# Transformer layers in one kernel: the PSUM banks of the projections divided five to three, and more score maxima computed there

## The chip, the cores and the metric

The kernel runs on one core of one Trainium2 chip. The metric is the device time of one execution in microseconds (us); the median of several runs is compared. An engine is named as in the profile: PE (TensorE matmul), PEld (its weight loads), DVE (VectorE), ACT (ScalarE), POOL (GpSimd) and SP (SyncE, which issues DMAs). PSUM, where PE puts its results, has eight banks of 128 x 512 fp32 each.

## The reference

One sequence of 2048 rows and 640 columns goes twice through an attention block and a dense block, with the same weights each time:

```
x = x + A(layernorm(x)); x = x + B(layernorm(x))     # twice
A: qkv = x @ wqkv; 32 heads of 20 columns each
   scores = q k^T / sqrt(20); p = softmax(scores over 2048 keys); (p v) @ wo
B: r = max(x @ w1 + b1, 0); (r * r) @ w2 + b2        # 1536 columns inside
```

The softmax needs, for each head and each query, the maximum over 2048 scores before the exponentials can be summed. The kernel computes it exactly, in a pass of its own.

## The kernel before

Each layer has three stages: the projections (`qkv`), attention (`attention`), and a dense stage (`add_heads`, `mlp`). Everything is written out in the order in which it is to run; each engine takes its instructions in that order and waits on semaphores where data or a bank is not ready.

**Projections.** There are 72 sums per layer: 40 for queries and keys (128 weight columns by 512 rows of x, named `("qk", tb, pos)`), then 32 for values (128 rows by 320 columns). Both operands are split in a high and a low part, so a sum takes 15 products (5 blocks of 128 x three combinations), and each product is cut in two halves of 64 rows of the array that work side by side, `r` 0 and 1. In `product` (L311) one half opens a sum with its 15 products, and the other half closes it with its own 15 into the same bank. A mark on ACT (L333) keeps the halves in order. In `work_on` (L893) the halves take turns: in each phase of 15 steps one half opens a sum while the other closes an earlier one, so that a sum opens in one phase, rests in the next, and is closed in the third. A sum gets its bank from the ring `ps_pj` (L97) when its first product is issued (L330). When it is closed, `end` (L859) has ACT read it: once (L263) or twice (L263 and L265) for queries and keys, once (L377) for values.

**Maxima in the projections.** Between these products `insert` (L810) puts matmuls of scores by queries (L481), whose maxima are needed later. They take their banks from the ring `ps_q` (L98). There are plain ones ("one": matmul, maximum on DVE, L493) and doubled ones, which deal with two blocks of keys at once: max(a, b) = b + relu(a - b). For these a first matmul with differences of keys goes through a relu on ACT ("step", L502), and a second is added to it, with the maximum, on DVE ("both", L510). A pair is put in only where a small model says that the next bank of the ring is free: `now` holds a clock for PE, DVE and ACT, `busy` a time for each bank, and `takes` (L768) advances them. The lists `PLAIN` and `DOUBLE` (L661, L667) say which blocks of queries and keys may be put in, and in what order; what does not fit by the end of the projections is left to attention.

**Attention.** A key tile of one block of 512 queries and 4 heads needs four score matmuls (L565, letters a and b for the two row halves), four exponentials on ACT (L572), and eight instructions on PE that sum the exponentials times the values (L577, letter V). The remaining maxima (L481, L493, letters m and n) are mixed in. `ORDERS` (L958) holds one order for each number of pairs of maxima in eight key tiles, 12 to 16; `pairs` (L1102) chooses the number from what is still due, at least 12.

Of the kernel before, what the change touches and what calls it, by code (L numbers as in the profile page):

```python
# [25 lines left out]
NQB = S // QB  # L26
# [13 lines left out]
def tile_layers(  # L40
# [53 lines left out]
            return [self.order[(self.n + 1 + i) % len(self.order)] for i in range(k)]  # L94

    ps_st = Ring(0, 1, 2, 3)
    ps_pj = Ring(4, 5, 6, 7)  # L97
    ps_q = Ring(0, 1, 2, 3)  # L98
    ps_all = Ring(0, 1, 2, 3, 4, 5, 6, 7)

    ident = cpool.tile([P, P], F32, name="ident")
# [321 lines left out]
    k_t, q_t, v_t, mx_t, kept = {}, {}, {}, {}, {}  # L423
# [65 lines left out]
    def smax(ring, t, p, sub, c, par):  # L489

        dst = ring("sm")
        by_queries(dst, t, p, sub, c, par)
        nc.vector.tensor_reduce(  # L493
            maxima(t)[:, 2 * par + p, sub, c : c + 1], dst, axis=AX.X, op=ALU.max
        )
# [58 lines left out]
    free = []  # L554
# [90 lines left out]
    def prep_job():  # L645
# [7 lines left out]
        if jobs:  # L653
# [16 lines left out]
        ([(0, 2, "d")], [(1, 2, "d")]),  # L670
        ([(0, 3, "d"), (0, 3, "e"), (0, 2, "e"), (0, 1, "e"), (0, 0, "e")],
         [(1, 3, "d"), (1, 0, "e"), (1, 1, "e"), (1, 2, "e"), (1, 3, "e")]
         + [(2, qb, c) for qb in range(NQB) for c in "de"]),
    ]
    PARTLY = {g * NQB + qb for x in DOUBLE for y in x for g, qb, c in y}

# [7 lines left out]
    def qkv(first, x_src, rest, scores):  # L684
# [5 lines left out]
        state = {"n": 0, "op": None, "last": "one", "scores": True}  # L690
        turning = []
        now = {"pe": 0.0, "dve": 0.0, "act": 0.0}
        busy = [0.0] * 8
# [8 lines left out]
        for pos in range(2 if first else FIRST, 10):  # L702
            n = UNITS.index((0, pos)) - 5 if pos >= FIRST else 0
# [9 lines left out]
        for k in range(KD if first else w_v.n):  # L713
            n = len(UNITS) - 8 + k
# [50 lines left out]
            while len(pending) > keep:  # L765
                pending.pop(0)()

        def takes(engine, ns, spot):  # L768
            now[engine] = max(now[engine], now["pe"] + 0.25) + ns
            busy[spot] = now[engine] + 0.12  # L770

        def choose():

# [12 lines left out]
        def single(op, par):  # L786

            (g, qb, x), p, sub = op["w"]
            t = g * NQB + qb
            spot = ps_q.coming(1)[0]  # L790
            if op["kind"] == "one":
                smax(ps_q, t, p, sub, x, par)
                takes("dve", 0.62, spot)
                keys_done = [x]
            elif op["kind"] == "step":
                op["r"].append(step_one(t, p, sub, x, par))
                takes("act", 0.58, spot)
                op["ready"].append(now["act"] - 0.2)
                return
            else:  # L800
                both_one(t, p, sub, x, par, op["r"][par])
                takes("dve", 0.7, spot)
                c = 2 * "de".index(x)
                keys_done = [c, c + 1]
            if par:
                done.update((t, p, sub, c) for c in keys_done)
                if (p, sub) == PAIRS[-1]:
                    end_group(op["w"][0])

        def insert(par):  # L810


            op = state["op"]
            if bool(op) != bool(par):
                return False
            if now["pe"] < max(busy[b] for b in ps_q.coming(1)):
                return False
            if turning and not par and now["pe"] >= turning[0][0]:
                if now["pe"] < max(busy[b] for b in ps_q.coming(2)):
                    return False  # L820
                now["pe"] += 1.2
                for spot in ps_q.coming(2):
                    takes("act", 0.6, spot)
                    takes("dve", 0.7, spot)
                step_turn()
                return False
            if not op:
                if min(at_now) >= (len(chains) - 1) * N + 2 * N // 3:
                    if state["scores"]:
                        state["scores"] = False  # L830
                        next(scores)
                    return False
                op = state["op"] = choose()
                if not op:
                    return False
                state["last"] = op["kind"]
            single(op, par)
            if par:
                state["op"] = None
            return True  # L840
# [8 lines left out]
        def step_turn():  # L849
            if next(turning[0][1], None) is None:  # L850
                turning.pop(0)
# [57 lines left out]
        for j in range(len(chains)):  # L909
# [18 lines left out]
            n = j - 2  # L928
# [31 lines left out]
        15: "anbmnanbaabmbnammbnaVbmbmmbVmbananVanmbanVnambmbVanbmnaVnmbaanVmbbanmV",  # L960
        14: "mbbbanmbbmambmVanannaVmbnaaanVbmabnmVanbmbmbVnaanmbVmabmbanVbmannaVn",
        13: "baanmbVmbanambbnbmVanbmnaVnaabnmbVanbmaanVnmbbanaVmnbmabVabbmmnaVm",
        12: "naambbmVanmbambVbmannabVnabnmabVabnmbanVbbmnanaVbmmbaanVbmbmnaaV",
    }

    def attention(first, x_src, first_rows):
# [4 lines left out]
        st_n, sm_n = [0, 0], [0, 0]  # L971
        state = {"begun": -1, "done": 0, "acc": None, "debt": 0}
        sm_ring = Ring(4, 5, 6)
        todo = [
            (t, p, sub, c)
            for t in range(NBLK)
            for c in range(4)
            for p, sub in PAIRS
            if (t, p, sub, c) not in done
        ]  # L980
# [13 lines left out]
        def begin(i):  # L994

            t, u = divmod(i, NKT)
            g, qb = divmod(t, NQB)
            if u == 1:
                q_t.pop(t - 1, None)
                if t + 2 < NBLK and t + 2 not in q_t:  # L1000
                    load_q(t + 2)
            if u % 4 == 1 and qb == 0:
                k_t.pop((g - 1, u // 4), None)
                for h in (0, 1, 2, 3) if g else (0, 1, 2):
                    if g + h < NG and (g + h, u // 4) not in k_t:
                        load_k(g + h, u // 4, True)
                if g and g + 3 >= NG:
                    del kept[(g - 1) % 4, u // 4]
            if t == 1 and u % 4 == 1:
                load_k(3, u // 4, True)  # L1010
            if u in (2, 10) and qb == NQB - 1 and g + 1 < NG:
                load_v(g + 1, u // 8)
            if first and t < 16 and u % 6 == 3:
                prep_job()
            if first and t < 16 and u == 8:
                for sp in (w_o, w_1, w_2):
                    sp.save_full()
                    sp.past(sp.count, sp.got)
            if (t, u) in loads:
                loads[t, u]()  # L1020
            if t == NBLK - 1 and u == 12:
                first_rows.extend(row_tile(x_src, i) for i in range(4))
            if i in split:
                split.pop(i)()
# [77 lines left out]
        def pairs():  # L1102

            n, i = min(sm_n), state["begun"] + 1
            most = max(
                [8 * (e + 1 - n) / max(t * NKT - 3 - i, 1) for t, e in ends.items() if e >= n],
                default=0,
            )
            state["debt"] += most
            n = min(max(int(state["debt"]), 12), 16)  # L1110
            state["debt"] -= n
            return n

        free.extend((5, 6))
        for o in "abab":
            op(o)
        yield
# [2 lines left out]
        spare = 0  # L1120
        while state["done"] < wide:
            for o in ORDERS[pairs()]:
# [3 lines left out]
                        both_heads(spare // 2 - 1)  # L1126
                else:
                    op(o)
        assert min(sm_n) == len(todo) and spare == 4
        for p in (0, 1, 0):  # L1130
            both_heads(p)
        while state["done"] < last:
# [11 lines left out]
    ready = {}  # L1144
# [348 lines left out]
```

## Time and profile before

| | |
|---|---|
| median of 3 runs | 3582.21 us (3581.59 to 3583.35) |
| profiled execution: span from first to last instruction | 3581.5 us (the page gives no other time for it) |
| granted PE clock | 1.000 |
| PE busy | 3569.0 us |
| DVE busy | 2753.5 us |
| ACT busy | 2647.3 us |
| POOL busy | 805.2 us |
| maxima matmuls L481 (plain and second of a doubled one; first of a doubled one) | 3586 of 427 ns, 510 of 400 ns |
| products of the projections L331 (queries and keys; values) | 2400 of 394 ns, 1920 of 307 ns |
| sums of attention L577 | 8192 of 605 ns |

A line "L331 PE" means instructions that line 331 of the kernel issued on PE. A busy time is the union of the spans of an engine's instructions. Matmuls overlap each other, since each is listed from its start to its result, so PE can be busy all the time without issuing at its fastest; the spacing of starts tells more. In the text, a window such as 700.00:790.00 is in us from the start of the span.

### The profile page before, as it was taken

The numbers are of one execution on the slowest core, as the hardware profiler recorded it, in microseconds if no ns is written. First come the engines' busy times: TensorE is split into PE (matmuls) and PEld (weight loads), VectorE is DVE, ScalarE is ACT, GpSimd is POOL, SyncE is SP. The second block draws the span as 40 slices with busy tenths as digits, with TensorE's granted clock in tenths as the row PEclk, the third lists the DMA queues.
The fourth block names the chain that finished last, engine by engine and source line by source line (L and its number), as shares of the span: only waits on it lengthen the run. The fifth ranks groups of instructions, "written<-read, shape, count | busy, mean of one in ns | idle before, by whom it ended". The sixth has DMA issues, their size and how long they took to land.

```text
span 3581.5 us, 67667 instructions
## 1 busy us (share of the span) xinstructions
PE 3569.0 (100%) x25560; PEld 2121.6 (59%) x25560; DVE 2753.5 (77%) x5085; ACT 2647.3 (74%) x5146; POOL 805.2 (22%) x880
## 2 busy tenths in 40 slices
PE   9999999999999999999999999999999999999999
PEld 7896343333334335999988954333334433369998
DVE  8778999999999993455567789999999999824443
ACT  3778999999999995122237789999999999942221
POOL 6531434211211211111153201211211211211110
PEclk9999999999999999999999999999999999999999
DMA  9765555323211136834477652232232211367221
GB/s 305 274 230 167 168 157 155 105 69 81 57 44 51 46 95 204 262 99 115 134 275 244 192 149 70 62 81 60 66 79 54 52 39 45 112 216 248 74 80 39
DMA packets 377397, 452.58 MB, mean 126 GB/s; under 512 B 176642, under 2 KB 223746, under 8 KB 377070
## 3 DMA queue, kind: packets, MB, share of 16 engines
q1 hardware_dynamic: 376254, 445.89, 41.6%
q8 instruction: 201, 3.29, 0.4%
q10 hardware_dynamic: 816, 2.36, 0.2%
q14 instruction: 126, 1.03, 0.1%
HBM read 273.83 MB, written 174.30 MB: 125 GB/s over the span
## 4 chain that ended last, share of the span: by engine, by line
PE 96%; DVE 2%; DMA 1%; issue 0%; ACT 0%; POOL 0%; SPq 0%; ACTq 0%; DVEq 0%
PE banks L577 28%; PE banks L565 20%; PE banks L481 16%; PE banks L293 13%; PE banks L331 10%; PE banks L1259 9%; DVE mx L493 1%; PE banks L1091 1%; DMA q<-d_qk 0%; ACT e L1098 0%; DVE bst L244 0%; DVE xnT L257 0%; DVE x L252 0%; DMA d_qk<-ev 0%; PE banks L408 0%
## 5 line engine op out<-in xcount | busy, mean ns | idle before, releaser
L572 ACT ACTIVATE e<-banks 128x512 f32<-128x512 f32 x3968 | 2049.4, 604 | 61.1 <-PE banks L481 1.7
L493 DVE TENSOR_REDUCE mx<-banks 128x1 f32<-128x512 f32 x3076 | 1929.6, 683 | 208.4 <-PE banks L481 137.2
L481 PE MATMUL banks<-k,q 60*128 60x512 f32 x3586 | 1244.3, 427 | 1.0 <-DMA q<-d_qk 0.5
L565 PE MATMUL banks<-q,k 62*128 62x512 f32 x3968 | 1118.7, 434 | 0.4 <-DVE mx L510 0.4
L577 PE MATMUL banks<-e,vg 128*32 128x512 f32 x8192 | 1091.0, 605 | 1.5 <-ACT e L1098 1.5
L565 PEld LDWEIGHTS banks<-q,k 62*128 62x128 f32 x3968 | 584.4, 185 | 657.8 <-ACT e L572 625.6
L481 PEld LDWEIGHTS banks<-k,q 60*128 60x128 f32 x3586 | 582.0, 184 | 283.1 <-DVE mx L493 210.8
L510 DVE CUSTOM_DVE_ANT_0 rl<-banks,rl 128x512 f32<-128x512 f32 x510 | 332.6, 688 | 101.6 <-PE banks L481 91.0
L331 PE MATMUL banks<-xnT,wqk 64*128 64x512 f32 x2400 | 379.7, 394 | 0.3 <-ACT mark_t L333 0.3
L1244 ACT ACTIVATE r<-banks,b_t 128x512 f32<-128x512 f32 x96 | 66.2, 689 | 419.7 <-PE banks L293 418.3
L577 PEld LDWEIGHTS banks<-e,vg 128*32 128x32 f32 x8192 | 161.1, 108 | 360.2 <-issue 333.1
L502 ACT ACTIVATE rl<-banks 128x512 f32<-128x512 f32 x510 | 270.8, 597 | 98.9 <-PE banks L481 93.6
L1259 PE MATMUL banks<-w,h 128*128 128x320 f32 x2304 | 340.4, 309 | 0.0
L1259 PEld LDWEIGHTS banks<-w,h 128*128 128x128 f32 x2304 | 339.2, 188 | 1.2
L293 PE MATMUL banks<-xnT,w 128*128 128x512 f32 x1440 | 329.4, 389 | 0.0
L331 PEld LDWEIGHTS banks<-xnT,wqk 64*128 64x128 f32 x2400 | 286.4, 185 | 34.3 <-issue 2.4
L293 PEld LDWEIGHTS banks<-xnT,w 128*128 128x128 f32 x1440 | 269.6, 188 | 55.3
L271 POOL CAST mr<-nt 128x32 fp32r<-128x32 f32 x64 | 13.4, 209 | 1143.5 <-DVE nt L536 1143.5
L621 POOL TENSOR_TENSOR few<-few,minus_t 128x16 f32<-128x16 f32 x62 | 179.8, 2900 | 215.6 <-DMA few<-d_s 213.7
L331 PE MATMUL banks<-wv,xnT 64*128 64x320 f32 x1920 | 199.2, 307 | 0.9 <-ACT mark_t L333 0.9
L331 PEld LDWEIGHTS banks<-wv,xnT 64*128 64x128 f32 x1920 | 186.5, 185 | 2.7 <-ACT mark_t L333 1.4
L1245 DVE TENSOR_TENSOR r<-r 128x512 f32<-128x512 f32 x96 | 74.3, 774 | 124.0 <-ACT r L1244 124.0
(86 smaller groups left out, 2010.8 us busy)
## 6 DMA issues: line engine op xcount, KB each, us to landing
q<-d_qk SPq DMA_DIRECT2D x242, 240.0 KB
d_qk<-ev SPq DMA_DIRECT2D x80, 512.0 KB
k<-d_qk SPq DMA_DIRECT2D x152, 240.0 KB
x<-d_x SPq DMA_DIRECT2D x84, 320.0 KB
d_qk<-ev SPq DMA_DIRECT2D x80, 256.0 KB
d_o<-ot SPq DMA_DIRECT2D x248, 80.0 KB
ot<-d_o SPq DMA_DIRECT2D x38, 512.0 KB
d_v<-v SPq DMA_DIRECT2D x32, 512.0 KB
```

The source lines that it names most:

```text
L293: nc.tensor.matmul(dst, a, b, start=(n == 0), stop=(n == last))
L331: m = nc.tensor.matmul(ch["dst"][:, :width], *pair, start=first, stop=last)
L481: nc.tensor.matmul(dst, q_t[t][b : b + 60, p, sub * P : (sub + 1) * P], k_t[t // NQB, c][b : b + 60, p, :], start=True, stop=True,)
L493: nc.vector.tensor_reduce(maxima(t)[:, 2 * par + p, sub, c : c + 1], dst, axis=AX.X, op=ALU.max)
L502: nc.scalar.activation(res, dst, AF.Relu)
L510: nc.vector.tensor_tensor_reduce(out=r, in0=dst, in1=r, scale=1.0, scalar=LEAST, op0=ALU.add, op1=ALU.max, accum_out=maxima(t)[:, 2 * par ...
L565: nc.tensor.matmul(dst, k_t[t // NQB, kt // 4][b : b + 62, p, (kt % 4) * P : (kt % 4 + 1) * P], q_t[t][b : b + 62, p, :], start=True, stop ...
L572: nc.scalar.activation(es[p][:, par, :], dst, AF.Exp, scale=SCALE)
L577: nc.tensor.matmul(acc[32 * h : 32 * h + 32, :], v_t[t // NQB, kt // 8][:, kt % 8, 32 * h : 32 * h + 32], es[p][:, par, :], start=(kt == 0 ...
L621: nc.gpsimd.tensor_tensor(few, few, minus_t, op=ALU.pow)
L1245: nc.vector.tensor_mul(r, r, r)
L1259: nc.tensor.matmul(dst[:, :HALF], hs[f][:, hx, i * P : (i + 1) * P], w_2.piece(at_2(f0 + f, hw, hf)), start=(f == 0 and (hx, hw) == THREE[0]),
```

## The change

It has four parts. The eight banks are divided anew: three (5, 6, 7) for the sums of the projections and five (0 to 4) for the maxima there. `DOUBLE` gets four more blocks (group 3, query blocks 0 and 1). The model behind `insert` charges an engine a spacing and a bank a whole duration, and begins no earlier than 0.44 us behind PE. And attention may choose ten or eleven pairs of maxima per eight key tiles, with an order for each.

```diff
-    ps_pj = Ring(4, 5, 6, 7)
-    ps_q = Ring(0, 1, 2, 3)
+    ps_pj = Ring(5, 6, 7)
+    ps_q = Ring(0, 1, 2, 3, 4)
...
-         + [(2, qb, c) for qb in range(NQB) for c in "de"]),
+         + [(2, qb, c) for qb in range(NQB) for c in "de"] + [(3, 0, "d"), (3, 0, "e"), (3, 1, "d"), (3, 1, "e")]),
...
-        def takes(engine, ns, spot):
-            now[engine] = max(now[engine], now["pe"] + 0.25) + ns
-            busy[spot] = now[engine] + 0.12
+        SPACING = {"dve": 0.60, "act": 0.48}
+        WHOLE = {"dve": 0.78, "act": 0.70}
+
+        def takes(engine, spot):
+            begins = max(now[engine], now["pe"] + 0.44)
+            now[engine] = begins + SPACING[engine]
+            busy[spot] = begins + WHOLE[engine]
+            return busy[spot]
...
-                takes("dve", 0.62, spot)
+                takes("dve", spot)
...
-                takes("act", 0.58, spot)
-                op["ready"].append(now["act"] - 0.2)
+                op["ready"].append(takes("act", spot) - 0.44)
...
-                takes("dve", 0.7, spot)
+                takes("dve", spot)
...
-                    takes("act", 0.6, spot)
-                    takes("dve", 0.7, spot)
+                    takes("act", spot)
+                    takes("dve", spot)
...
+        11: "ananmbbVmbanmabVmbabmnaVbabmnaVbmbmnaaVnabnmbaVnabanmbVabanmbV",
+        10: "anmbabVabmnmbaVmbabanVbmnanabV" * 2,
...
-            if t == 1 and u % 4 == 1:
+            if t == 1 and u % 4 == 1 and (3, u // 4) not in k_t:
...
-            n = min(max(int(state["debt"]), 12), 16)
+            n = min(max(int(state["debt"]), 10), 16)
...
-        free.extend((5, 6))
+        free.extend((ps_pj.coming(1)[0], 4))
...
-        assert min(sm_n) == len(todo) and spare == 4
+        assert min(sm_n) == len(todo) and spare >= 4, spare
```

The change moves instructions. The first place is PE in the first layer's projections of queries and keys, where one sum closes and the next opens. xnT is a block of the input, wqk of the weights; "waits Activation" is a semaphore of ACT. Before, the third last row closes a sum in bank 6, and the last row opens the next one in bank 5 (as the ring gives them out), with no wait:

```order
L331 MATMUL banks_74<-xnT53_456,wqk169_1592 128x512
L331 MATMUL banks_74<-xnT97_802,wqk169_1592 128x512
L481 MATMUL banks_74<-kd111_1005,q160_1522 128x512 [waits DVE_49]
L331 MATMUL banks_74<-xnT97_802,wqk169_1592 128x512
L331 MATMUL banks_74<-xnT53_456,wqk169_1592 128x512
L331 MATMUL banks_74<-xnT75_616,wqk139_1320 128x512
L331 MATMUL banks_74<-xnT24_251,wqk169_1592 128x512
```

Now, the second row closes a sum in bank 6, and the sixth opens the next one in the same bank, behind ACT's read of it:

```order
L481 MATMUL banks_74<-kd112_1012,q167_1559 128x512 [waits Activation_49]
L331 MATMUL banks_74<-xnT28_263,wqk180_1644 128x512
L331 MATMUL banks_74<-xnT80_642,wqk180_1644 128x512
L481 MATMUL banks_74<-k71_591,q167_1559 128x512 [waits Activation_49]
L331 MATMUL banks_74<-xnT47_419,wqk140_1332 128x512
L331 MATMUL banks_74<-xnT91_766,wqk140_1332 128x512 [waits Activation_49]
L481 MATMUL banks_74<-k71_591,q167_1559 128x512 [waits DVE_49]
```

Over both layers 138 sums open in a bank that an earlier sum of the same projections had. Before, 31 to 55 matmuls of PE lie from the closing one to the opening one, and 18 openers name a wait for such a read; now the distance is 2 for 88 of them, 4 for 43, 6 for 6 and 10 for one, and 135 openers wait for the read (L263, L265 or L377) of the bank that they open. Of the 138, 56 banks were read once for queries and keys (29 openers at distance 2, 26 at 4, 1 at 6), 24 twice (17, 4, 2, and 1 at 10), and 58 for values (42, 13, 3).

The maxima matmuls in the projections go from 572 to 678 in the first layer and from 576 to 680 in the second, all of the added ones doubled.

The second place is PE in attention, in the middle of the first layer. Before, each key tile has four scores (L565) and three maxima (L481) ahead of its sums (L577):

```order
L565 MATMUL banks<-q_9329,k_5325 128x512
L481 MATMUL banks<-k_4962,q_9476 128x512
L565 MATMUL banks<-q_9329,k_5325 128x512
L481 MATMUL banks<-k_4962,q_9476 128x512 x2
L565 MATMUL banks<-q_9329,k_5325 128x512 x2
L577 MATMUL banks<-e_4746,vg_8849 32x512 x2
L577 MATMUL banks<-e_4745,vg_8849 32x512 x2
```

Now some key tiles have two maxima:

```order
L565 MATMUL banks<-q_10154,k_4742 128x512 x3
L481 MATMUL banks<-k_5156,q_10161 128x512 x2
L565 MATMUL banks<-q_10154,k_4742 128x512
L577 MATMUL banks<-e_5028,vg_10341 32x512 x2
L577 MATMUL banks<-e_5027,vg_10341 32x512 x2
```

In each layer 104 key tiles now have two and 387 three, where 491 and 489 had three before. In groups of eight key tiles eleven and twelve pairs occur, ten does not. The other stages keep their instructions.

## The prediction

> **What bounds the kernel now.** I read the page first: busy time by engine and the chain of work that ended last.
>
> ```profile
> span 3581.5 us, 67667 instructions
> PE 3569.0 (100%) x25560; PEld 2121.6 (59%) x25560; DVE 2753.5 (77%) x5085; ACT 2647.3 (74%) x5146; POOL 805.2 (22%) x880
> PE 96%; DVE 2%; DMA 1%; issue 0%; ACT 0%; POOL 0%; SPq 0%; ACTq 0%; DVEq 0%
> PE banks L577 28%; PE banks L565 20%; PE banks L481 16%; PE banks L293 13%; PE banks L331 10%; PE banks L1259 9%; DVE mx L493 1%; PE banks L1091 1%; DMA q<-d_qk 0%; ACT e L1098 0%; DVE bst L244 0%; DVE xnT L257 0%; DVE x L252 0%; DMA d_qk<-ev 0%; PE banks L408 0%
> ```
>
> PE is the bound of every stage. Its modelled ends hide short gaps, so I then counted matmuls per stretch: one with projections of queries and keys, one with projections of values, one of attention (columns: PE, PEld, DVE, ACT, POOL, clock, DMA share, GB/s).
>
> ```profile
> 1870.00:1910.00 40.00, 40.00 (x337) 32.69 (x336) 32.40 (x96) 28.82 (x61) 18.36 (x19) 1.00 0.79 276
> 2030.00:2074.00 44.00, 44.00 (x538) 43.04 (x534) 32.68 (x102) 31.91 (x79) 2.09 (x5) 1.00 0.74 210
> 700.00:790.00 90.00, 90.00 (x640) 35.74 (x634) 81.79 (x135) 87.48 (x171) 16.21 (x15) 1.00 0.28 72
> ```
>
> In the projections a matmul starts every 40/337 = 0.119 us (512 columns) and every 44/538 = 0.082 us (values: 320 columns, mixed with maxima). Two row halves work side by side, so one lasts over three times the spacing:
>
> ```profile
> L331 PE MATMUL banks<-xnT,wqk x2400: 383/392/502, 12.3 to 1994.3; 64*128 64x512 f32 x185
> L331 PE MATMUL banks<-wv,xnT x1920: 299/306/413, 206.9 to 2090.5; 64*128 64x320 f32 x192
> ```
>
> There is hardly a stall in the projections to be filled. What is added to PE there costs time, and so does what makes PE wait there.
>
> **The change, part 1: three banks for the sums.** A sum (a chain, in the code) is opened by one row half, rests for a phase, and is closed by the other half. So during each phase one sum is open, one rests and one closes: three banks. With a ring of four, the next sum opens in the fourth while ACT reads the closed one. With three, it opens in the bank that has just been closed. The order shown ahead says how far opener and closer are apart: of the 138 openers that reuse a bank inside a projection, all but the first few now stand 2 (88 times), 4 (43), 6 (6) or 10 (1) matmuls behind the closer of the same bank, where they stood 31 or more before. 135 of them wait for ACT's read of that bank. PE takes its instructions in order, so all that stands behind waits too: the other half's products and the inserted maxima.
>
> How long is that wait? Here a closing run of products, the reads that follow it on ACT, and PE's answer to an ACT instruction at the end of attention, where PE visibly waits:
>
> ```profile
> 1834.51 0.86 PE L331 MATMUL banks<-xnT,wqk 64*128 64x512 f32 x5
> 1835.47 0.59 ACT L263 COPY r<-banks 128x512 f32<-128x512 f32 x1
> 1835.95 0.59 ACT L265 CAST ev<-banks 128x512 fp32r<-128x512 f32 x1
> ...
> 1391.78 1.43 ACT e L1098
> 1393.20 0.04 issue
> 1393.25 1.06 PE banks L577 x8
> ...
> L377 ACT COPY v<-banks x60: 409/426/449, 219.2 to 2085.6; 128x320 f32<-128x320 f32 x60
> ```
>
> The closer ends at 1834.51 + 0.86 = 1835.37, the read begins 0.10 us later and takes 0.59; a second read (the first four column blocks of the weights, in three of four row blocks) begins 0.48 later. PE answers 0.05 us after ACT's end. After a wait PE also loses about 0.10 us, since the first two pairs stand 0.34 us apart and not 0.235; this is seen behind every switch to attention's sums:
>
> ```profile
> 699.60 1.07 PE L577 MATMUL banks<-e,vg 128*32 128x512 f32 x8
> 700.59 0.50 PE L565 MATMUL banks<-q,k 62*128 62x512 f32 x1
> 700.93 0.39 PE L565 MATMUL banks<-q,k 62*128 62x512 f32 x1
> 701.17 0.62 PE L565 MATMUL banks<-q,k 62*128 62x512 f32 x2
> 701.72 1.07 PE L577 MATMUL banks<-e,vg 128*32 128x512 f32 x8
> ```
>
> So from closer's start to opener: 0.39 + 0.10 + 0.59 + 0.05 + 0.10 = 1.23 us with one read, 1.71 with two, and 0.31 + 0.10 + 0.43 + 0.05 + 0.10 = 0.99 for values. Taken off is what PE needs anyway over 2, 4 or 6 places.
>
> - One read, 56 openers: 29 x (1.23 - 0.24) + 26 x (1.23 - 0.48) + 1 x (1.23 - 0.71) = 28.7 + 19.5 + 0.5 = 48.7 us.
> - Two reads, 24: 17 x 1.47 + 4 x 1.23 + 2 x 1.00 + 1 x 0.52 = 32.4 us.
> - Values, 58: 42 x (0.99 - 0.16) + 13 x (0.99 - 0.33) + 3 x (0.99 - 0.49) = 34.9 + 8.6 + 1.5 = 45.0 us.
>
> That is 126 us for both layers. Two corrections have opposite signs. ACT is busy 28.82 of 40 us, and a relu that it has begun delays the read by up to 0.60 us: if one closer in six meets a whole one, 14 us more; one in three, 28. On the other side, some ten openers fall into the first 50 us of the kernel, where PE waits for its inputs anyway (8 us), and PE's present waits for a free bank of the maxima (rows like the one below) go where PE comes later (up to 14 us).
>
> ```profile
> 1874.34 0.18 PEld L481 LDWEIGHTS banks<-kd,q 60*128 60x128 f32 x1 [0.20 <-DVE mx L493]
> ```
>
> I let them cancel: 126, with bounds 104 and 154.
>
> By the Trainium skill, "TensorE: Matmul & The Clock Gate", section "Architectural detail: the array is 16× 32×32, not 1× 128×128", PE's queue can pull weight loads ahead of matmuls in flight, which would take the 0.10 us of each restart away and leave 126 - 14 = 112. The row at 700.93 speaks against it: whatever was pulled ahead, the second pair came 0.34 us after the first. That row stands behind a switch to another kind of matmul, not behind a wait for a bank, so it is the nearest row and no proof; I keep the 0.10.
>
> **Part 2: more maxima in the projections.** Per layer 104 matmuls of L481 move from attention to the projections (576 to 680 in the second layer), as 52 pairs of a relu on ACT and a combined maximum on DVE where attention had 104 plain maxima. PE's price is 208 x 0.119 = +24.7 us over both layers. On DVE 104 operations of 0.69 us (L510) more, on ACT 104 of 0.60 (L502); both lie beside PE, since DVE is busy 32.40 and ACT 28.82 of 40 us and PE gets slower. If they were not covered, the maxima would wait, not the sums.
>
> ```profile
> L502 ACT ACTIVATE rl<-banks 128x512 f32<-128x512 f32 x510 | 270.8, 597 | 98.9 <-PE banks L481 93.6
> L510 DVE CUSTOM_DVE_ANT_0 rl<-banks,rl 128x512 f32<-128x512 f32 x510 | 332.6, 688 | 101.6 <-PE banks L481 91.0
> ```
>
> The fifth bank for maxima only lets them stand earlier in the order. Twelve more DMAs in 2500 land on queues that no PE row of these stretches waits for; I cost them at nothing.
>
> **Part 3: attention with eleven.** Every key tile had four scores and three maxima; now 104 of some 490 key tiles per layer have two. Ten pairs are never chosen, only eleven and twelve. A key tile takes 2.12 us (699.60 to 701.72): 1.0 for its sums, 0.34 to the second pair, then pairs at 0.235. Seven matmuls put four on one row half and three on the other, so they fill four places; six fill three. The most that two maxima can save is one place, 0.235. The least comes from the key tiles after the last maximum, where ACT's four exponentials set the pace:
>
> ```profile
> 1356.08 1.06 PE L577 MATMUL banks<-e,vg 128*32 128x512 f32 x8
> 1358.08 1.06 PE L577 MATMUL banks<-e,vg 128*32 128x512 f32 x8
> 1360.15 1.06 PE L577 MATMUL banks<-e,vg 128*32 128x512 f32 x8
> ```
>
> Four scores alone take 2.00 and 2.07 us, only 0.09 less than 2.12. But a shorter key tile has three longer ones around it in which ACT catches up, so I take 0.20: 208 x 0.20 = -41.6 us, with bounds 0.09 (-19) and 0.235 (-49).
>
> **Sum.** 126 + 24.7 - 41.6 = +109 us on the profiled span of 3581.5, which is 3690.6. The runs' median of 3582.21 lies 0.7 above that span, so about **3691 us**. With the bounds: 104 + 25 - 49 = +80 and 154 + 25 - 19 = +160.
>
> **Rivals.**
>
> - *Not slower.* The price is paid only if PE stands still. If the openers found their banks free, attention's gain would exceed the added maxima: 24.7 - 41.6 = -17, 3565 us. The place is the opener; it decides at 17/138 = 0.12 us of waiting each. Against it: a read alone takes 0.59 us, and two or four places are 0.24 or 0.48.
> - *Only half of the wait shows.* While one row half waits for the bank, the other goes on with what is already in the array, and half of the 126 is won back: 63 - 17 = +46, 3628 us. For it: an opener at a distance of four lets through maxima of the other half. Against it: at 1393.25 all of PE had stood still. The Trainium skill, "TensorEngine Tiling (Array Packing)", section "Key Properties", says that different tiles load and multiply in parallel, which would favour this rival; it does not say that one queue passes a waiting instruction.
> - *ACT becomes the bound at the openers.* With more relus the read stands behind a full one each time: 138 x 0.60 = 83 in place of none, +192, 3774 us. For it: at 1903.39 to 1904.62 ACT read a closed bank straight behind two relus (row below). Against it: each wait of PE lets ACT run dry.
>
> ```profile
> 1903.39 1.10 ACT L502 ACTIVATE rl<-banks 128x512 f32<-128x512 f32 x2
> 1904.62 0.59 ACT L263 COPY r<-banks 128x512 f32<-128x512 f32 x1
> ```
>
> - *The clock falls.* Pauses of about 1 us every five could lower PE's granted clock. If the projections, 292 us in the second layer (from the first row below to the last L331 at 2090.5) and about as long in the first, ran at half speed for half of their work, that would add 292 us to the 109: 3983 us. Against it: the clock stays at 1.00 where attention ends with a wait in each key tile (below). The Trainium skill, "TensorE: Matmul & The Clock Gate", section "A second HAM failure mode: psum-queue depth-cycling", tells of a kernel whose small pauses between groups in cycled banks did this.
>
> ```profile
> 1798.08 3.64 PE banks L331 x29
> ...
> 1350.00:1440.00 90.00, 89.05 (x597) 58.32 (x590) 30.33 (x56) 43.59 (x60) 9.56 (x15) 1.00 0.65 209
> ```
>
> **How the numbers follow.** The forecast has 0.78, the half-hidden wait 0.08, ACT as the bound 0.08, not slower 0.04, the clock 0.02. Bounds of +80 to +160 give 3662 to 3742; I widen to 3640 and 3750, to hold part of the second and third case. A measurement of this kernel can hardly tell 0.2% (7 us) from no change. Faster by more than that: 0.03, most of the not-slower case; within it: 0.02; slower: 0.95.
>
> **What would show it.** In the profile of the changed kernel: weight loads of L331 that wait for L263, L265 and L377, about 135 times, some 0.5 to 1.5 us each, in sum about 110 to 140 us; a PE that is no longer at 100% in the projections, with spacing near 0.14 us per matmul; a second layer whose projections end some 70 us later after their start; attention shorter by about 20 us per layer, key tiles with two maxima of 1.9 us; granted clock 1.00 throughout. It would be wrong if such waits are few or short, if they stand at ACT's relus instead, or if the added time lies in attention.

## The result and the profile after

The changed kernel takes 3726.88 us (median of 4 runs, 3726.57 to 3728.21), the kernel before 3582.78 us beside it (4 runs, 3581.59 to 3583.76). The ratio is 1.0401, with a 95% interval of 1.0387 to 1.0416: 144 us slower, where 109 had been forecast. The page of the profiled execution opens with the span, the busy times, and the busy tenths of 40 slices:

```profile
span 3725.0 us, 68406 instructions
...
PE 3609.4 (97%) x25566; PEld 2131.2 (57%) x25566; DVE 2695.7 (72%) x5089; ACT 2681.2 (72%) x5254; POOL 804.6 (22%) x880
...
PE   8988999999999999999988889999999999999999
...
PEclk9999999999999999999999999999999999999999
```

PE falls from 100% to 97%, and the slices with an 8 lie in the two stretches of projections. The clock row stays at 9 there. The same kind of stretch as before (queries and keys of the first layer, of the second layer, values, attention; columns: PE, PEld, DVE, ACT, POOL, clock, DMA share, GB/s):

```profile
100.00:140.00 40.00, 36.08 (x287) 28.39 (x289) 32.37 (x92) 25.50 (x55) 20.08 (x22) 1.00 0.70 239
1940.00:1980.00 40.00, 35.38 (x283) 28.56 (x279) 31.22 (x86) 21.71 (x47) 17.72 (x18) 1.00 0.79 268
2180.00:2224.00 44.00, 36.79 (x408) 33.31 (x406) 26.31 (x82) 25.72 (x60) 1.25 (x3) 1.00 0.47 141
700.00:790.00 90.00, 90.00 (x636) 35.76 (x636) 77.60 (x128) 87.72 (x173) 24.55 (x26) 1.00 0.36 111
```

In the projections a matmul now starts every 40/283 = 0.141 us (0.119 before) and every 44/408 = 0.108 us in the values (0.082 before). ACT is less busy there than before (21.71 of 40 us against 28.82): PE waits for ACT, and ACT in turn waits for PE. What PE's products waited for, first in the kernel before and then in the changed one (idle us of PE and of PEld ahead of L331, added up, and how often; the longest rows):

```profile
  ACT mark_t L333: 3.5, 6
  issue: 2.4, 14
```

```profile
its engine sat idle before it (us, times) until:
  ACT v L377: 73.7, 87
  ACT mark_t L333: 69.9, 64
  ACT r L263: 64.0, 77
  ACT ev L265: 55.6, 47
  issue: 2.4, 14
```

PE's and PEld's idle time is counted one after the other here, so the sum of 263 us is no loss of time. Nor is L333, the mark of the row halves, a releaser of its own: ACT runs it just ahead of a read or just behind it. Taken opener by opener, all 138 openers start 0.053 or 0.054 us behind the end of ACT's read of their bank. One of them, of values, in the timeline (start, duration, engine, line; in brackets the wait):

```profile
2186.87 1.57 ACT L502 ACTIVATE rl<-banks 128x512 f32<-128x512 f32 x3 [1.68 <-PE banks L331]
2186.88 0.60 PE L331 MATMUL banks<-wv,xnT 64*128 64x320 f32 x5
2188.31 0.17 ACT L333 COPY mark_t<-mark_t 1x1 f32<-1x1 f32 x1
2188.39 0.41 ACT L377 COPY v<-banks 128x320 f32<-128x320 f32 x1
2188.86 0.42 PE L331 MATMUL banks<-wv,xnT 64*128 64x320 f32 x2 [1.37 <-ACT v L377]
```

The product that closes the sum is one of the five in the second row; it starts at 2187.04 and ends at 2187.34. ACT is then in the first of three relus of maxima and works through all of them before it reads the bank, at 2188.39, 1.05 us after the closer's end. The read ends at 2188.80, and PE, which has stood still, opens the next sum at 2188.86.

Where the 143.5 us of span come from, by the gaps from one start on PE to the next, both layers together:

| | before, us | after, us | difference, us |
|---|---|---|---|
| gaps ahead of the openers (71 per layer) | 15.7 | 155.8 | +140.1 |
| the two gaps behind each opener | 30.1 | 43.0 | +12.9 |
| all other gaps of the projections | 545.0 | 558.8 | +13.8 |
| projections, first to last product | 590.8 | 757.6 | +166.8 |
| from there to attention's first sum | 3.4 | 5.0 | +1.6 |
| attention, first to last sum | 2162.2 | 2137.2 | -25.0 |

The sum is +143.4, the last three rows added. The dense stages are unchanged.

### The profile page after: what moved, and what is told of

Its sections match the earlier page's. It is cut to its first block, busy times and chain, and to the rows that moved or that the text cites. A ratio compares the mean times of both kernels' runs of the same rounds, so it can differ in the third digit from the quotient of the medians.

```text
span 3725.0 us, 68406 instructions
## 1 busy us (share of the span) xinstructions
PE 3609.4 (97%) x25566; PEld 2131.2 (57%) x25566; DVE 2695.7 (72%) x5089; ACT 2681.2 (72%) x5254; POOL 804.6 (22%) x880
## 3 DMA queue, kind: packets, MB, share of 16 engines
q14 instruction: 131, 1.07, 0.1%
## 4 chain that ended last, share of the span: by engine, by line
PE 57%; ACT 2%; issue 1%; DMA 0%; DVE 0%; POOL 0%; SPq 0%; ACTq 0%; POOLq 0%; DVEq 0%
PE banks L577 14%; PE banks L293 13%; PE banks L1265 9%; PE banks L565 9%; PE banks L481 8%; PE banks L331 5%; ACT r L263 0%; ACT rl L502 0%; ACT v L377 0%; PE banks L1097 0%; ACT mark_t L333 0%; DVE rl L510 0%; DMA q<-d_qk 0%; ACT ev L265 0%; ACT e L1104 0%
## 5 line engine op out<-in xcount | busy, mean ns | idle before, releaser
L493 DVE TENSOR_REDUCE mx<-banks 128x1 f32<-128x512 f32 x2872 | 1810.6, 684 | 320.7 <-PE banks L481 206.7
L565 PE MATMUL banks<-q,k 62*128 62x512 f32 x3968 | 1138.5, 433 | 0.8 <-DVE mx L510 0.6
L481 PE MATMUL banks<-k,q 60*128 60x512 f32 x3484 | 1109.7, 423 | 1.6 <-DVE v L377 1.6
L577 PE MATMUL banks<-e,vg 128*32 128x512 f32 x8192 | 1091.0, 605 | 1.5 <-ACT e L1104 1.5
L565 PEld LDWEIGHTS banks<-q,k 62*128 62x128 f32 x3968 | 546.2, 185 | 505.7 <-ACT e L572 457.4
L481 PEld LDWEIGHTS banks<-k,q 60*128 60x128 f32 x3484 | 536.1, 185 | 452.1 <-DVE mx L493 390.2
L510 DVE CUSTOM_DVE_ANT_0 rl<-banks,rl 128x512 f32<-128x512 f32 x612 | 391.0, 688 | 184.3 <-PE banks L481 156.9
L502 ACT ACTIVATE rl<-banks 128x512 f32<-128x512 f32 x618 | 326.9, 604 | 198.0 <-PE banks L481 176.7
L331 PE MATMUL banks<-xnT,wqk 64*128 64x512 f32 x2400 | 404.6, 399 | 55.4 <-ACT ev L265 22.8
L331 PEld LDWEIGHTS banks<-xnT,wqk 64*128 64x128 f32 x2400 | 286.5, 186 | 123.0 <-ACT r L263 36.4
L577 PEld LDWEIGHTS banks<-e,vg 128*32 128x32 f32 x8192 | 161.2, 108 | 326.3 <-issue 304.3
L331 PE MATMUL banks<-wv,xnT 64*128 64x320 f32 x1920 | 221.5, 313 | 50.6 <-ACT v L377 29.5
L331 PEld LDWEIGHTS banks<-wv,xnT 64*128 64x128 f32 x1920 | 194.0, 185 | 72.9 <-ACT v L377 44.1
L481 PE MATMUL banks<-kd,q 60*128 60x512 f32 x618 | 198.9, 403 | 0.0
```

The lines of the kernel that those rows point to most:

```text
L331: m = nc.tensor.matmul(ch["dst"][:, :width], *pair, start=first, stop=last)
L481: nc.tensor.matmul(dst, q_t[t][b : b + 60, p, sub * P : (sub + 1) * P], k_t[t // NQB, c][b : b + 60, p, :], start=True, stop=True,)
L493: nc.vector.tensor_reduce(maxima(t)[:, 2 * par + p, sub, c : c + 1], dst, axis=AX.X, op=ALU.max)
L502: nc.scalar.activation(res, dst, AF.Relu)
L510: nc.vector.tensor_tensor_reduce(out=r, in0=dst, in1=r, scale=1.0, scalar=LEAST, op0=ALU.add, op1=ALU.max, accum_out=maxima(t)[:, 2 * par ...
L565: nc.tensor.matmul(dst, k_t[t // NQB, kt // 4][b : b + 62, p, (kt % 4) * P : (kt % 4 + 1) * P], q_t[t][b : b + 62, p, :], start=True, stop ...
```

## The experiments

Eight kernels were run, each timed against the kernel before on the same chip (3584.34 us beside the first four described here, 3583.42 us beside the other four).

**The three banks undone.** The changed kernel with four banks for the sums and four for the maxima again:

```diff
-    ps_pj = Ring(5, 6, 7)
-    ps_q = Ring(0, 1, 2, 3, 4)
+    ps_pj = Ring(4, 5, 6, 7)
+    ps_q = Ring(0, 1, 2, 3)
...
-        free.extend((ps_pj.coming(1)[0], 4))
+        free.extend((5, 6))
```

> The changed kernel with the old division of banks, four for the sums and four for the maxima (and attention's first two scores back in banks 5 and 6); the new lists, the new model and the orders for ten and eleven stay. 650 and 658 maxima matmuls then stand in the projections, 76 and 84 key tiles of attention have two maxima. If the wait of each opening product for the read of its bank is the cause, it is gone: 160 added matmuls x 0.119 = +19 us, 160 key tiles x 0.148 (measured in the changed kernel) = -24, so about 3577 us, between 3568 and 3590. If the denser maxima are to blame, it stays above 3680.

Measured: 3593.4 us, ratio 1.0025 (1.0016 to 1.0034). The banks are worth 133 to 135 us of the 144 (3726.88 - 3593.4, or 144 - 9). The windows of the second layer's projections and of attention:

```profile
1940.00:1980.00 40.00, 40.00 (x341) 36.75 (x340) 35.49 (x109) 32.49 (x70) 14.66 (x16) 1.00 0.74 253
700.00:790.00 90.00, 90.00 (x638) 35.81 (x630) 77.99 (x130) 87.50 (x171) 19.53 (x18) 1.00 0.33 89
```

PE is full again, with 341 matmuls in 40 us. Yet this kernel is not the 3577 us that I had expected, but 9 us slower than before. It has 160 more maxima matmuls in the projections (1308 against 1148). The projections became 26.1 us longer (616.9 against 590.8), 0.163 us per moved matmul and not 0.119; attention became 17.2 us shorter, 0.107 us per moved matmul. So even with the banks left alone, a maximum costs more in the projections than it saves in attention.

**The three banks alone.** The kernel before with nothing but the banks changed (the same three lines the other way):

> The kernel before with the new division of banks alone (three for the sums, five for the maxima). 138 opening products stand 2 to 6 matmuls behind the closing one of their bank (109 at 2). If the wait for the read is the cause: 138 x about 1.0 us = +138, 64 more maxima matmuls x 0.119 = +8, some 20 key tiles without maxima at the end of attention x 0.12 = -3: about 3725 us, between 3700 and 3750. If the added maxima are to blame for the loss, below 3630.

Measured: 3737.96 us, ratio 1.0429 (1.0414 to 1.0443). What L331 waits for in it:

```profile
  ACT r L263: 73.5, 96
  ACT mark_t L333: 71.8, 60
  ACT v L377: 67.1, 78
  ACT ev L265: 60.3, 48
```

The same waits, with the old model of `insert` and no new orders in attention, whose length is that of before (1080.4 and 1080.5 us). The two experiments together put the whole loss on the division of the banks: with it alone +154, without it +9.

**Three banks, but no opener behind a closer.** Is it that the banks are few, or that the next sum opens in the bank just closed? Here one row half opens all sums and the other closes all of them, 15 + 6 steps behind, so that a bank does not rest for a phase between. The banks stay three and five.

```diff
+        N, at_now, LAG = 3 * KD, [0, 0], 6
...
+            if r and at_now[0] < min(at_now[1] + N + LAG, len(chains) * N):
+                return
...
-            if r == 0:
-                n = s ^ 1
-            elif s in (0, len(chains) - 1):
-                n = s
-            else:
-                n = s + 1 if s % 2 else s - 1
-            opens = n % 2 != r
+            opens = r == 0
```

> The changed kernel with its three and five banks, but one row half opens every sum and the other closes every sum, 15 + 6 steps behind, so that a closed bank has some nine steps (2.1 us) until the next sum opens in it. If the loss is the wait of an opening product directly behind the closing one, it is gone: 234 more maxima matmuls x 0.119 = +28, 236 key tiles x 0.148 = -35, 6 more half-filled steps per layer = +3, fewer waits of maxima for a bank (up to -10): about 3573 us, between 3560 and 3595. If three banks are too few whatever the order, or if the maxima are to blame, above 3650.

Measured: 3598.17 us, ratio 1.0038 (1.0025 to 1.0050). The list for L331 has no wait for a read left:

```profile
its engine sat idle before it (us, times) until:
  issue: 2.4, 14
  ACT xnT L256: 0.9, 3
  DVE xnT L257: 0.2, 1
```

The openers stand 21 or more matmuls behind the closer, and though ACT reads as late as in the changed kernel (0.44 us behind the closer for values), all but one find the bank free. Three banks are enough; the order that opens in the bank just closed is what costs. The expected 3573 was missed by 25 us: at the start of each layer's projections only the opening half works, and at the end only the closing one, so that 34 and 31 products follow one of the same half (1 and 0 before), and 1382 maxima are in the projections (1148 before). The 65 products stand 0.20 us apart and not 0.12, which is about 5 us. The 234 more maxima, at the 0.163 us of the first experiment instead of 0.119, are another 10, and attention became 28 us shorter where 35 had been expected. These do not quite add up to 25; the rest was not traced.

**No relus at the end of a phase.** If the reads are late since ACT is in a relu, then no relu just before the closer should take the lateness away and leave the read itself. In the changed kernel no maximum is begun in the last five steps of a phase:

```diff
+                if at_now[0] % N >= N - 5:
+                    return False
                 op = state["op"] = choose()
```

> The changed kernel, but no maxima are begun in the last five steps of a phase, so that ACT has fewer relus in front of it when a sum closes. 592 maxima matmuls stand in each layer's projections, 20 and 16 key tiles have two maxima. If relus ahead of the read are why the waits are longer than forecast, the read begins some 0.1 us behind the closing product's end (0.51 us for values and 0.32 for queries and keys read once, as measured in the changed kernel), and the sum of the waits at the opening products falls by 35 us or more from 156: with 174 fewer maxima matmuls (-21) and 172 fewer short key tiles (+25) about 3690 us. If the delay has another cause (the mark, the semaphore), it stays at 0.5 and 0.3 us, and the time at about 3731.

Measured: 3657.82 us, ratio 1.0206 (1.0192 to 1.0220): 69 us less than the changed kernel. Here a value opener as it is in that kernel:

```profile
2083.77 0.74 PE L331 MATMUL banks<-wv,xnT 64*128 64x320 f32 x7
...
2084.70 0.41 ACT L377 COPY v<-banks 128x320 f32<-128x320 f32 x1
2085.16 0.41 PE L331 MATMUL banks<-wv,xnT 64*128 64x320 f32 x1 [0.26 <-ACT v L377]
```

The closer is the last of the seven products in the first row; it ends at 2084.52, and the read starts 0.18 us later, with no relu in front. PE waits 0.26 us here, where it had waited 1.37. Over all openers the gaps ahead of them fall from 155.8 to 84.9 us. By the bank's kind:

| from closer's end to the read, us | forecast | changed kernel | three banks alone | no relus at the end |
|---|---|---|---|---|
| one read (56) | 0.10 | 0.32 | 0.22 | 0.11 |
| two reads (24) | 0.10 | 0.14 | 0.16 | 0.14 |
| values (58) | 0.10 | 0.50 | 0.52 | 0.11 |

Without relus in front (none of the 138 reads has one there), the delay is 0.11 to 0.14 us, close to the forecast's 0.10. So the relus make up the difference, and that is about 34 of the 71 us (56 x 0.21 + 58 x 0.39). The time fell by more than I had expected for a second reason: with maxima kept from the last steps they gather behind the closer, so that most openers of one-read banks stand 6 or 8 matmuls behind it (36 and 15 of 56) and not 2 or 4, and for values 34 stand at 4. More of the wait is then spent on useful work. It has fewer maxima in the projections (592 per layer), so attention is as long as before (1082.3 and 1079.8 us).

**ACT in attention.** A key tile with two maxima takes 1.980 us in the changed kernel and saves 0.146 us, not 0.20. One in the timeline, from one tile's sums to the next:

```profile
432.14 5.17 ACT L572 ACTIVATE e<-banks 128x512 f32<-128x512 f32 x10
432.69 1.07 PE L577 MATMUL banks<-e,vg 128*32 128x512 f32 x8
433.69 0.29 PEld L565 LDWEIGHTS banks<-q,k 62*128 62x128 f32 x3 [0.84 <-ACT e L572]
...
434.69 1.06 PE L577 MATMUL banks<-e,vg 128*32 128x512 f32 x8
```

ACT runs on without a break, ten exponentials in 5.17 us: four take about 2.0 us, as long as the tile. To test this, the exponentials of attention were made shorter: 384 of 512 columns, so that the other columns are summed with what earlier tiles left there.

```diff
-        nc.scalar.activation(es[p][:, par, :], dst, AF.Exp, scale=SCALE)
+        w = QB if len(e_n) <= 6 else 384
+        nc.scalar.activation(es[p][:, par, :w], dst[:, :w], AF.Exp, scale=SCALE)
```

> The changed kernel with less work for ACT in attention: after the first uses of each buffer the exponentials take only 384 of the 512 columns of a score (the last 128 columns of the weights keep old values, so that part of the softmax is not computed). PE's and DVE's work is the same. If ACT's four exponentials set the time of a key tile with two maxima (1.980 us in the changed kernel), it falls to the three places of PE, about 1.89 us, and a key tile with three stays near 2.126: 208 x 0.09 + 774 x 0.006 = -23, about 3704 us. If PE's order sets it, it stays at 1.98 and the time at 3727.

Measured: 3708.66 us, ratio 1.0351 (1.0335 to 1.0366), 18 us less than the changed kernel. The same tile:

```profile
432.33 1.07 PE L578 MATMUL banks<-e,vg 128*32 128x512 f32 x8
434.23 1.06 PE L578 MATMUL banks<-e,vg 128*32 128x512 f32 x8
```

Tiles with two maxima now take 1.900 us (208 of them), and tiles with three stay at 2.132. So ACT sets the tile with two maxima, and not the one with three. One place less for PE, as I had priced the upper bound, would be there if ACT were faster: 2.126 - 1.900 = 0.226 us.

**The new model alone.** The kernel before with only the new `takes` and its calls (four banks each, the old lists and orders):

```diff
-        def takes(engine, ns, spot):
-            now[engine] = max(now[engine], now["pe"] + 0.25) + ns
-            busy[spot] = now[engine] + 0.12
+        SPACING = {"dve": 0.60, "act": 0.48}
+        WHOLE = {"dve": 0.78, "act": 0.70}
+
+        def takes(engine, spot):
+            begins = max(now[engine], now["pe"] + 0.44)
+            now[engine] = begins + SPACING[engine]
+            busy[spot] = begins + WHOLE[engine]
+            return busy[spot]
...
```

> The kernel before with the new model of insertion alone: four and four banks, the old lists, at least twelve pairs per eight key tiles. 650 and 658 maxima matmuls stand in the projections, as in the kernel with four banks of before; in attention every key tile has three maxima until there are none left. The projections should take as long as there (311.9 and 305.0 us), attention should lose the gain of the eleven-pair orders except some 25 more key tiles without maxima at its end (25 x 0.13 = 3 us per layer): about 5 us per layer more than that kernel, 3603 us, between 3597 and 3609. If the orders with eleven bring nothing, 3593.

Measured: 3605.38 us, ratio 1.0061 (1.0046 to 1.0076). The model puts in 1308 maxima, as many as the kernel with the banks undone (3593.4 us), and its projections are as long (618.4 against 616.9 us). But attention still asks for at least twelve pairs per eight key tiles, uses its maxima up early and ends with 87 tiles without any, which take about 1.97 us, where it had 35 before. So the orders with eleven pairs (and the longer list that comes with them) are worth some 12 us where more maxima are put in, and less than the 26 us that putting them in costs.

**Fewer maxima in the projections.** If a maximum costs more in the projections than it saves in attention, fewer in the projections might win. The kernel before with a shorter list (448 per layer) and orders for 13 and 14 pairs that spread the additional ones:

```diff
-          [(1, 3, "d"), (1, 0, "e"), (1, 1, "e"), (1, 2, "e"), (1, 3, "e")]
-          + [(2, qb, c) for qb in range(NQB) for c in "de"]),
+          [(1, 3, "d"), (1, 0, "e"), (1, 1, "e")]),
...
```

> The opposite of the change: the kernel before with four blocks fewer in the lists (448 maxima matmuls in each layer's projections, not 572 and 576), and orders for thirteen and fourteen pairs in which a key tile has three or four maxima and four matmuls at most on each row half. 150 key tiles per layer then have four maxima. If a key tile costs as many places of PE as its fuller row half has matmuls (four with three maxima, four with four), attention gets no longer, and the projections lose 252 x 0.16 = -40 (0.16 measured for a moved maximum with four banks): about 3545 us. If the fourth maximum waits for one of the three banks that DVE clears in 0.6 us each, or DVE becomes the bound (4 x 0.61 = 2.46 us against 2.126), such key tiles take 2.3 to 2.5 us: +26 to +56 per layer, 3595 to 3655.

Measured: 3792.44 us, ratio 1.0584 (1.0568 to 1.0599); both expected numbers were missed. The projections became 15 and 17 us shorter, 32 together where 40 had been expected, but attention 121 us longer in each layer. In the timeline a tile with four maxima:

```profile
701.95 1.07 PE L577 MATMUL banks<-e,vg 128*32 128x512 f32 x8
702.95 0.50 PE L481 MATMUL banks<-k,q 60*128 60x512 f32 x1
703.29 0.73 PE L481 MATMUL banks<-k,q 60*128 60x512 f32 x2
704.23 0.49 PE L481 MATMUL banks<-k,q 60*128 60x512 f32 x1
704.65 1.06 PE L577 MATMUL banks<-e,vg 128*32 128x512 f32 x8
```

And what L481 waited for in this kernel:

```profile
  DVE mx L493: 830.3, 1343
  DMA k<-d_qk: 56.1, 4
```

From 701.95 to 704.65 is 2.70 us where a tile with three takes 2.13. Eight matmuls fill four places as seven do; the fourth matmul waits for a bank that DVE is still reading (830.3 us of such waits in the whole kernel, 213.5 before, those of PE and PEld added up). DVE is busy 2.68 of these 2.70 us, so the wait shows DVE's own pace at least as much as a want of banks; no run here tells the two apart. 150 tiles at +0.58 us make 87 of the 121 us per layer. The rest is 21 us in tiles with three, and a wait of about 14 us for keys at the start of attention.

The same with the orders for 13 and 14 of the kernel before:

> The same with the orders for thirteen and fourteen pairs that the kernel before already has (key tiles of uneven size, up to eleven matmuls ahead of one V). By places, thirteen old pairs take 5 tiles of 4 and 3 places like the others; DVE has 26 x 0.61 = 15.9 us of work in 17.0. Projections -40 as in the sister kernel, attention between -3 and +40 us per layer: if the places decide, 3540 to 3550; if banks and DVE decide, above 3590.

Measured: 3787.13 us, ratio 1.0567 (1.0550 to 1.0585), with attention 1202.2 and 1198.5 us long. In these orders the letters of two tiles run into one another, and with the shorter list this kernel does not compute the reference's result, by a cause in the order that I did not trace; so only its time is read. It is as long with other orders, which would speak for the price of the maxima and against the particular order as the cause. But its clock was lower: the granted clock in its attention is 0.97 and 0.98 in the two layers, and 1.00 with the new orders. By the trace's clock record it ran at half clock for 96 us there, which can be worth up to 48 us. So the equal times do not settle it.

None of the versions beats the kernel before. It stands between two losses: more maxima in the projections, at 0.16 us each against 0.11 saved, and more in attention, at about 0.6 us for each additional one in a tile.

## Why the prediction was right or wrong

**The mechanism and the direction** held: 3726.88 us lies inside the range of 3640 to 3750 us, at the upper end, and the waits are where they were forecast, at weight loads and matmuls of L331 behind L263, L265 and L377. I had expected 135 of 138 openers to wait and all 138 do. PE's answer, forecast at 0.05 us, measured 0.053 us; the loss at the restart, 0.10, measured 12.9/138 = 0.093 us, though the row for it stood behind another kind of switch. All of PE stands in the gap, maxima and the other half included. The rival in which half of the wait is hidden is refuted by the gaps themselves: +140 us against its 63. By the Trainium skill, "TensorE: Matmul & The Clock Gate", section "Step-by-step: what each phase is for", PE's queue may pull weight loads ahead while "The MATMULs themselves stay in program order". At the waits the trace agrees, since no matmul passed any of the 138 openers. Elsewhere it does not quite: around 260 us of the changed kernel, a matmul of one row half starts at 259.45 us, and three of the other half that stand ahead of it in the program start at 259.66 us and later. So the order is shown for the waits alone.

**The opener's wait** was forecast at 126 us and measured 140.1 + 12.9 = 153.0, at the upper bound of 154. The step that failed is "the read begins 0.10 us later", taken from a closer with no relu in front of the read. It measured 0.32, 0.14 and 0.50 us for the three kinds: 56 x 0.22 + 24 x 0.04 + 58 x 0.40 = +36 us. The added relus are not to blame: counted in the same way, the delay in the kernel before was already 0.29, 0.09 and 0.42 us in the mean (it cost nothing there, since the opener took another bank). So the profile of before had the right term, and the one row taken from it did not stand for the others. I had seen this term and priced it at 14 to 28, but let it cancel against early openers and against waits of the maxima. The early openers took nothing off: the nine that stand in the first 65 us cost 1.3 us each, like the others of their kind. That the miss is 27 us and not 36 is not accounted for. By kind, the gaps with the restart measured 58.3, 30.6 and 64.2 us, where 48.7, 32.4 and 45.0 stood: the values are the worst mis-sized, and there two or three relus run ahead of the read in 24 of 58 cases (18 of 56 with one read, none of 24 with two). The reasoning against the rival in which ACT is the bound, "each wait of PE lets ACT run dry", was the wrong half: ACT runs dry during the wait, but PE has then given it several relus straight before the closer, and it runs through these first. That rival was partly true, at 36 us and not at 83, though not by its reason of more relus.

**The added maxima** were forecast at +24.7 us. All gaps of the projections but the openers' grew by 13.8 us for 210 more matmuls, 0.066 us each, where a moved one costs 0.163 us with four banks for the maxima, by the first experiment. The 0.066 is no price of a maximum, since late starts went away at the same time: if a gap of 0.24 us or more (a pair of products takes 0.235) is called late, the late ones fell by 10 us and the others grew by 23. This is the correction that I had called "waits for a free bank of the maxima go where PE comes later", with up to 14. The split depends on where the line is drawn; with 0.30 us it is 7 and 20.

**Attention** was forecast at -41.6 us and measured -25.0. The step that failed is "a shorter key tile has three longer ones around it in which ACT catches up": ACT does not get ahead. As I read it, that is because the scores that it reads are made in the tile itself; no run tests this reason. The tile with two maxima takes 1.980 us, and 208 x 0.146 = -30; the 774 tiles with three cost 0.006 us more each, +5, and by the experiment with shorter exponentials this is not ACT's. What makes these 0.006 us is open. Per tile, 0.146 lies midway between the lower bound of 0.09, from four scores alone, and the 0.20 that I took; the sum of -25 is nearer to the lower bound's -19.

**The clock** stayed at 1.00. That rival is refuted for this kernel; that pauses of this length never lower the clock is not shown, as the last section tells.

**The sum** by the measured terms: 153.0 + 13.8 + 1.6 - 25.0 = +143.4 against 109: 27 us of the miss lie in the opener's wait and 17 in attention, and the maxima with the late starts that fell give 11 back. Without the 11 the time would still lie inside the range.

**Missed by the prediction altogether** was the balance of the change without its banks: I had it at 24.7 - 41.6 = -17 (the rival "not slower"), and it is +9 by the first experiment, with 160 maxima moved and not 208.

## What to carry to other kernels

When a buffer is taken from a ring, look at how far its last reader's release and its next writer stand apart in the program, not at how many buffers are in use at once; in these kernels three banks cost 4% with opener and closer mostly 2 or 4 matmuls apart, and 0.4% with 21 or more. An engine that reads such a buffer in order adds everything that stands ahead of the read in its queue: price the wait as read time plus that backlog, and take the backlog from the queue just ahead of the event, not from the engine's mean load. And a place that PE saves is only worth what the next engine leaves: compare it with the pace of that engine in the same tile first.

## What the runs showed of the hardware that had not been expected

A read's end to the waiting matmul's start took 0.053 or 0.054 us in all 138 cases of the changed kernel, whatever the read's length. The pauses of that kernel, about 1.1 us every five and 1.51 us at most, did not lower the granted clock, while one pause of about 14 us did, in the kernel with fewer maxima where attention starts (windows of 20 us):

```profile
290.00:310.00 20.00, 19.48 (x151) 9.89 (x152) 1.53 (x6) 15.98 (x34) 0.87 (x4) 1.00 0.85 266
310.00:330.00 20.00, 6.30 (x36) 1.69 (x28) 1.29 (x2) 5.29 (x11) 2.39 (x3) 0.62 0.73 184
330.00:350.00 20.00, 19.90 (x128) 7.76 (x128) 16.93 (x28) 16.69 (x33) 4.79 (x6) 0.95 0.12 28
```

The clock is 0.62 in the window in which PE is busy for 6.30 of 20 us, 0.95 in the next and 1.00 after that, until the same wait in the second layer. The Trainium skill, "TensorE: Matmul & The Clock Gate", section "HAM oscillation — how this bites in real kernels", gives 3.4 us as the length of an idle gap from which the clock falls. These two kernels agree with it, and a third does not. In attention of the kernel with the old orders for 13 and 14, the longest pause of PE is 1.32 us between the waits for keys, and yet the clock falls there 22 times, for 3.4 or 6.8 us each. All 22 begin within 4 us behind the start of a pause of 0.8 to 1.3 us, like this one (timeline, then a window behind it):

```profile
401.93 0.50 PE L481 MATMUL banks<-k,q 60*128 60x512 f32 x1
403.74 1.93 PE L577 MATMUL banks<-e,vg 128*32 128x512 f32 x8 [1.31 <-ACT e L572]
...
404.00:410.00 6.00, 6.00 (x28) 1.84 (x21) 2.03 (x4) 1.63 (x4) 3.16 (x5) 0.53 0.53 147
```

The granted clock is 0.53 in the window, and eight sums take 1.93 us where they take 1.07 at full clock. Other pauses of 1.31 us in the same kernel were followed by no fall. So the length of the single pause does not decide it, the measurement goes before the page here, and what does decide it is open.
